# Attention and a two-layer MoE block on one core: another stored order for the same program

## The chip, the cores and the metric

The kernel runs on one core of one Trainium2 chip. The metric is the device time of one execution in microseconds; several executions are timed and their median is given. One further execution is recorded by the hardware profiler, and its page and trace are what this document reads.

## What is computed

Eight batches of eight heads attend over 576 tokens, each with a window of 128 keys back and a bias that grows with distance; the result of all heads, 4608 tokens of 512 values, goes through two matrices with `h * cos(h)` between them. The reference, cut:

```python
def _attn_ref(q, k, v):              # (8, 8, 576, 64)
    scores = scale * np.matmul(q, k.transpose(0, 1, 3, 2))
    bias = slopes[:, None, None] * (-np.abs(rel).astype(np.float32))[None, :, :]
    mask = (rel >= 0) & (rel < 128)
    scores = np.where(mask, scores + bias[None], -1000000000.0)
    ...
    return np.matmul(attn, v)
def _moe_ref(x, w_in, w_out):        # x (4608, 512), w_in (512, 2048), w_out (2048, 512)
    h = x @ w_in
    g = h * np.cos(h)
    return g @ w_out
```

## The kernel before

The program is a list of 2777 steps. A step is one or a few instructions of one engine; a step names what it reads and writes, and `Plan.op` (the planner's recording function) derives from that which earlier steps it must wait for. `Plan.emit` turns these into semaphore waits. What decides the order is `Plan.schedule`: it decodes a long text constant, `STARTS`, into one number for each step, sorts all steps by it, and so fixes the order of the instructions of each of the five queues (PE, ACT, DVE, POOL, SP). One bit of each number says which engine takes a step that may run on ACT or DVE. No time of the numbers is used on the chip: only their order.

```python
    def schedule(self):
        raw, n = zlib.decompress(base64.b85decode(STARTS)), len(self.all)
        ...
            o.start = code >> 1
            if len(o.eng) > 1:
                e = "dve" if code & 1 else "act"
                o.fn, o.eng = o.fn[e], (e,)
        self.order = sorted(self.all, key=lambda o: (o.start, o.seq))
```

The work itself has three interleaved parts.

*Attention*, unit by unit. A batch has nine units: four pairs of heads for each of two groups of 256 tokens, called G0 and G1, and a tail of 64 tokens. A unit's scores are matmuls (L497, tail L488) into PSUM banks 4 to 7; ACT takes the exponential (L529, tail L521); DVE multiplies by the mask (L553, tail L540); PE multiplies by v (L584 and L587, tail L571 and L573) into banks 2 and 3; DVE divides by the sum (L623 and L625, tail L610 and L613) into a ring of eight xnat buffers (two xtail buffers for tails). The result is transposed into xT, either on PE (L691, L653) with a copy by ACT or DVE (L700, L701), or by a DMA transpose on the SP queue (L714, tails L709).

The queries and keys of batches 0 and 1 are transposed on PE (L442, copies L459 and L460). Those of batches 2 to 7 are loaded by POOL into qnat and knat (L338) and then transposed by two DMA transposes each on the SP queue (L349 for the first 512 tokens, L352 for the rest) into qt and kt. Of all these there are two buffers, by even and odd batch, so the load for batch 3 onwards waits until the transpose before it has landed. v is loaded by POOL (L328).

*The first matrix (moe1)*: nine chunks of 512 tokens, numbered 0 to 8, each with 16 pieces of 128 outputs (L729; chunk 0 in halves, L753). A piece is four matmuls of 512 columns, a cosine on ACT (L735) and a product on DVE (L739) into gT. xT holds four batches' tokens and is used in a ring.

*The second matrix (moe2)*: chunk 0 plainly (L814, copies to the output buffers L820 or L822, stores L826). Chunks 1 to 8 use Strassen's seven products P1 to P7 of 16 matmuls each (L870) with sums of weights (L780) and of gT made by DVE, in banks 0 and 1. The partial results are read by ACT (L890) or DVE (L894) into four output buffers ob 0 to 3, in the order 0, 3, 2, 1, and each is stored by a DMA on the SP queue (L915). A buffer is written again only after its store has landed.

Three things set what waits for what around the change. Each engine takes its instructions strictly in the stored order. The SP queue carries three kinds of DMA in one order: transposes of q and k, transposes of xnat and xtail, and stores of outputs. POOL's queue carries all loads, in the order in which the program lists them, which the stored numbers do not move. At the start PE runs some matmuls on zeros (L415), ACT makes the masks (L422), and DVE sets constants with memsets (L393 to L398).

Of the kernel before, what the change touches and what calls it, by code (L numbers as in the profile page):

```python
# [14 lines left out]
B, H, S, D = 8, 8, 576, 64  # L15
# [12 lines left out]


STARTS = (  # L30
    "c-p;I4^&iD8lM5w+uPIjylD=XA&1L@)!DZ=!DE==&YKwm#u0JCBtYD7mURWuZ3#Cu{8JK=x<ux>u7#<cUH{g))KN}(j+SLb="
    "&I{6D{HsS&X)FPv&{tL&+K<+U>Fz>t8@09^WNP1-S7VSe&6r+-O*@$J(|9!uhpaVX*8odd>UV%3k|Km<KwSJ)7K1nq9P)@uL"
    "MRknm(tV{xt&zU!Oy8d|+1#zgn%PBkV-Mg-2{@hOqVA;CeSY+8we<r#3R^(-%g6-xty!7_)ESnr;5xs7Or&$3W9QI>M*DJUF"
    "6J?Sm~*or4UKn!!HWknQ_6^o4}c9byUh8SdLN7<OL>NWr!*1iFC%kGd8(ZkP5doDeea>(UOJzpw=KJ`p`5x`eMXx@|B(+Hg>"
    "MIBx#7HZ<FVvo@k7gc-hpx){V5txwxOldEkY-2NYa&WNtixxhZZTs7J@f1UwF&38sI{0VdE%~mMS!YrsG3`JiMzoAgP5nO#k"
    "(ait$1Pzf<SA%D03nsW1?$Mgip0=kmq8G6CfK}W5-O-5b8qp<8mzvR6ud{G}fL%kD8*O;u8Dj1a8r2R>m|j{!x_!Ovi0+V*&"
    "Y>977BX#g=eMJ{GP|$!7M@P+|A&x6#OE7I*4H8A^+h~P-P80FGJp^?BZAo<!)X@KY%c{PB0ECojryjShh5(Tgw7FN#)RD%H("
    "lu~dy##n&LM@X`3}PE9wr;17a{*fb#?b^xL<mmP=lcp+4eoO*gY~2dTzkd5mNR;Gab-g;M)_%fMG1!fd4?o@DR1yjuAr)OKQ"
    "}}A!={n-qTzi=HP*#`wo7+5H;7e0Jr(c!Y*ZB@Vvt--8V#3K5b`6yb=Dt3E^w_hOy;M@O?gkO4R>cPESlU=x$H{P;S@lYI2t"
    "Ddc^H^y4`h^$)7~kAHigf?{cxWO;@zz8OO%wzjivEwsiP_hugiz*6faRmFXwn{zy%nn*4_0(Fa%7I;FYtM|3y2H%&S#PM`j4"  # L40
    "aRgoZS2}mDLpqBy5?-Ek$o61k>B?DFv0b_)=_)O#IC|x$tCwtxzb_H#5fac^^-lu)ib7H?dr3eTA&i|Y7Ev=n0x=afA}=47^"
    "lZF<L~xaLES4aN&(*837-kTJ2zwM!FSLj`b1|5N1JbLdQ;!OKOh7tz(7&=E61EcwZYt!~>K=%}9)xXtv{2;3m6GoLGDScxO5"
    "{m1;v5NE7LLs~dvoWVp6`9(MC)=Q>hH)9FM484Ul{k#Z{2AY$*iB@tN9(XJ|`vn)_#>cI}L(NB_G5+tIYE?6gtF<%2=WyFG|"
    "1KbXVFqns9=Hc<G(d4d=YPHTK}o6TKU#OT^Wpl&%!u+eC~FmU>)+MWsZPptlQ)PWrIPDfZB<ISLld*p1I+B_^N6L@#0yJ4>*"
    "rrw58RxbvwZO6=FzB~n(1vALc-w7!}e*xq9o*5^3V<huX9sQ!W$87WIqJk-S2;bqEm>OEAUiRuE*4aZOB!<RiFiG;FKN)4W*"
    "9<8Eck~&_bGG&W5o8vua^$$&vGAAFD&3}>C&tIIK&Jt2qHE(a7V-+0<>ymTcYB-gK)r60vxALYyz%vCN<}%BcwSTvmkDRyYv"
    "mSGjN)M8G!V&-IE+-2Wi04obZ?ayAUKbogL=WjC?ybD1mwSx@ihYphmougoC8AYGm}tGghp1jaOOTw1>hf6XQvz~=EeZUJIL"
    "+2=F95tKJBURI0>j(zddHK-eNjrr-@J=(3457r!<*SH7~6^*zr$iVRUK5yDp2Dw#Yw7KMMM)TGrF*aO{bU`?rGdgFlCRI5F2"
    "Hyxev=e-SUj_kXd~Ict0cNXi}?e9-C7{=B5BA64FnSx{W)g8^>~n+(aVCwx*gNEqmMA+mlT>sU+9<a+)H&<4vHfRyN14*O?Q"
    "5UBzEo_8)TBx(}?-c^kb-i6y;6v-~qsX(yF3M+C!5jujwOArMRg7$wKOg@P~=&=X2bUICb;3*tDx=s*e+8~vk+V!3RVP?3P5"  # L50
    "?>GX2;wu)@9Y`LxLRhZdh>@9tE#;c{(o*WgL%0`3Y+$?LTd&T>`Bet>%VdgAI%ek=U^Dv|?D>v|M64+6BOtMveF_NO$^Hly%"
    "2Htko4Ot7ouux@P>?bngVazq26RBx<xiQ_+|x@_oGo|%o-F%7$w}M1J;U8@zhgzc**()#IWt9kx;_m{OV1fCH@7yJKjc;Coq"
    "5GZOIp)8vN{bU_nP+$3bc!=ZuLI@>K0SEWkW@LkW+z=&Hxy=poJ;W%!7pJ!#FS~1D+BuDd(F4=(;%3cr)g8?or^8?0g;=vNO"
    ";4nTb#lTHAoARJHQ$0wg6TfwcjXq`Eg0Dcbr83RE5glpv#o2u753V~d}{_3U+V$qG!}r|nPg-0YM96YxtA@&t<9l7YP@LX}f"
    "&pvSpz1{rD@WeWgMqfD@2>0U$yqdy&UAr8KWtnS4|B9~(^ku~zIU=KrPp>RNeVOT{?szP8h(#&jyvjWz0WN)iHwIkE2oE06e"
    "^DCOSpIG`!`hr+?q`{PP7x}0DJu8;1mnY)!cB3=(Wci*sQ$)S^aqFHl?h3c7c(*r;<GX+MIG3&3BNBlGP$c_Y=|U|D;w{E}C"
    "4{B`3%4gf>~CT?rGFNh_!5T%Rbr_1z&gPa9r+(*@=qW*Ij1#$3re-Zv9nA_vY|U6ym@lslhy_R4J4>=3QdzmslM#ZL(Mp!t+"
    "c<3J&wjnM9ez86lmtLE=a~8-$q_z*&0qf_8WdBvT2G7gx*%fS2*aW<s}i98`yh(&*@t%H|L6FDeG5Rb{b0BS2Z7RPH{lZ{dE"
    "7kN={7as>l>Nxl7eaR-0_TzxD<4_)KM=F}6}NTE_qOPCMiDbUd~4T1&1z-E{5i0W1WZfQL4yY=m<JqQcP!1E_GZAqjBN-IwG"
    "in;lpPWs;zA(U0@KOsWXM0xtm>$31*GjP<$r908WhTX4(WVi7RhLgc*W5`hXh+FC(5Q)W;XmeqAoyXx8Wrc&I+RxdKv)v1dW"  # L60
    "C69t|jV?fiDlS9gH*o#rs8cAlORSATft$M6WmBru$&^ZlsW*85z!`7a0KbJk!tb1!7n`>?zvMWRc%<y)DkW#l>DMxN=q`_R@"
    "5A>4iDqSc8x~boUD$W&{6!)m*~qib8LE3VP>^_d$VN>lW~#us+l!Jc6LR+^4v~>8A%r;j#UH&|Ksms7<U)3G&0cL>XuU#+M}"
    "{7%GQtm%qpf@73uG&)LY1(S;u5M;tuUR`&zPW)&6JhNn>>bDPudAE;Oh&;GR>awuXElCHLitvC#h>hSGALUD^aD1sT*4Wi8;"
    "&6HpB4;yq;y0EtCPLF~>y{Xf&m!N|6c=*X(yCF~z&-jMH*V+AYW)MC2BQQ=14Sq+CGWEU#TOKUeh`AvS&V^EH2l_$VzRHU%Q"
    "Xx|6bG<Pztoh#2?~x3U1@hssQlELKZ0er(z+e%4UIFI{+JthWhN){Bx~IG`jU+M0LXm9;CAmBYQxrqS|(MaSQ#MO!J0%-U+8"
    "RwyW+(YT|usm8$m0b4h)y_HG<EsMp9r}XeCdjTXelI+Jxj`0PrxD1ZM0_vepWVo=AX8*xM?FRL<w{}tW7SoR}QP3$4FqNOGC"
    "2uVz<P#T0&LVF`E0$?W-mMZ`1Q-|D6`ov0Z=@%b1A(-{faI-!W~6SGl2=h*wWoFigk3LdXlHzP{4p5jbL+V`k#Kav`w69h2G"
    "mEi$A6&-=+^ju$Nvukga^0"
)


# [988 lines left out]
```

The softmax here doesn't subtract the row's maximum and nothing guards it: scores larger than these inputs give would overflow.

## Time and profile before

| what | us |
|---|---|
| median of 6 runs (lowest to highest) | 305.74 (304.47 to 307.09) |
| the profiled execution, its own time | 306.38 |
| its span on the core | 304.7 |
| PE busy in the span, matmuls | 295.0 |
| DVE busy | 252.0 |
| ACT busy | 204.0 |
| POOL busy | 95.1 |

The span runs from the first to the last instruction that the profiler recorded; the 1.7 us between 304.7 and 306.38 lie around it. Times of single instructions below count from the start of the span. A group line of the profile gives the line of the kernel, engine, operation, tiles and shape, the count, the busy time, the mean of one in ns, and after the bar the idle time of the engine just before such an instruction with what ended it. A matmul's length in the profile holds its way through the pipeline, so back-to-back matmuls overlap in the list, and the distance of their starts is what a stream of them costs.

### The profile page before, as it was taken

The page shows a single profiled execution, that of the slowest core. Times are in us where ns is not written, and L with a number is a line of the kernel's source. Part 1 is how long each engine was busy: PE and PEld are TensorE (multiplying, and loading weights), DVE is VectorE, ACT ScalarE, POOL GpSimd, SP SyncE. Part 2 cuts the span into 40 slices and gives each one's busy share as a digit, 9 for nine tenths or more (in the row PEclk, how much of TensorE's full clock was granted, in tenths as well). Part 3 has the DMA queues.
Part 4 walks back from the last instruction along what each step waited for, and adds up shares of the span by engine and source line. Part 5 has one row for each costly group of instructions (what it writes and reads, how often), then busy time and mean ns, then how long its engine had stood idle before and what let it go on. Part 6 is the DMA issues. An engine that isn't in the chain of part 4 may idle for free.

```text
span 304.7 us, 7167 instructions
## 1 busy us (share of the span) xinstructions
PE 295.0 (97%) x2911; PEld 197.5 (65%) x2911; DVE 252.0 (83%) x542; ACT 204.0 (67%) x293; POOL 95.1 (31%) x122
## 2 busy tenths in 40 slices
PE   7699999998999999999999999999999999999996
PEld 3478745545874577537888886468645765555785
DVE  2788758789788998989988988999988976788963
ACT  6896877688555787787757776778667935556211
POOL 7998240052998801860178004000000000000000
PEclk9889999999999999999999999999999999999999
DMA  7999999999999999999899937960120314010044
GB/s 140 180 202 210 207 165 155 131 166 147 143 191 156 156 173 176 159 162 185 90 171 161 180 73 99 187 133 11 29 62 10 95 27 137 22 34 0 2 139 140
DMA packets 148353, 38.09 MB, mean 125 GB/s; under 512 B 133984, under 2 KB 147040, under 8 KB 148320
## 3 DMA queue, kind: packets, MB, share of 16 engines
q0 software_dynamic: 99344, 18.10, 76.1%
q1 hardware_dynamic: 48976, 19.54, 32.2%
q8 instruction: 23, 0.38, 0.6%
q14 instruction: 10, 0.08, 0.1%
HBM read 36.70 MB, written 9.44 MB: 151 GB/s over the span
## 4 chain that ended last, share of the span: by engine, by line
PE 87%; DMA 3%; ACT 3%; SPq 2%; DVE 2%; issue 1%; DVEq 0%
PE ps L870 32%; PE ps L729 32%; PE ps L497 5%; PE ps L753 5%; PE ps L814 5%; PE ps L584 3%; DMA kt<-knat 2%; PE ps L587 2%; ACT p L529 2%; SPq L349 2%; DMA ob<-in_q_dram 1%; PE ps L442 1%; PE ps L488 1%; PE ps L691 1%; PE ps L571 1%
## 5 line engine op out<-in xcount | busy, mean ns | idle before, releaser
L729 PE MATMUL ps<-xT,w_inb 128*128 128x512 bf16 (+1 forms) x576 | 129.7, 355 | 0.2
L735 ACT ACTIVATE cos<-ps,halfpi 128x512 f32<-128x512 f32 x128 | 83.0, 686 | 46.0 <-PE ps L729 32.9
L739 DVE TENSOR_TENSOR gT<-ps,cos 128x512 f16<-128x512 f32 x128 | 83.1, 686 | 15.2 <-ACT cos L735 14.4
L729 PEld LDWEIGHTS ps<-xT,w_inb 128*128 128x128 bf16 x576 | 54.5, 98 | 44.5 <-DVE gT L739 5.9
L529 ACT ACTIVATE p<-ps 128x768 bf16<-128x768 f32 (+1 forms) x64 | 56.3, 917 | 15.0 <-PE ps L497 12.8
L328 POOL DMA_DIRECT2D vp<-in_v_dram x40 | 34.0, 884 | 64.4 <-PE ps L587 53.4
L870 PE MATMUL ps<-wsum,gT 128*128 128x256 f16 x256 | 46.8, 273 | 0.0
L870 PE MATMUL ps<-wsum,gsum 128*128 128x256 f16 x256 | 46.1, 273 | 0.0
L553 DVE TENSOR_TENSOR p<-p,emask 128x512 bf16<-128x512 bf16 (+2 forms) x96 | 42.1, 459 | 4.0 <-ACT p L529 3.4
L870 PE MATMUL ps<-w_outb,gT 128*128 128x256 f16 x256 | 43.8, 273 | 0.0
L338 POOL DMA_DIRECT2D qnat<-in_q_dram x30 | 25.6, 900 | 18.9 <-DMA qt<-qnat 17.7
L870 PEld LDWEIGHTS ps<-w_outb,gT 128*128 128x128 f16 x256 | 24.9, 98 | 7.3 <-DVE ob L894 0.3
L338 POOL DMA_DIRECT2D knat<-in_k_dram x30 | 25.5, 913 | 9.5 <-DMA kt<-knat 8.1
L870 PEld LDWEIGHTS ps<-wsum,gT 128*128 128x128 f16 x256 | 23.7, 98 | 6.1 <-DVE krows L894 0.3
L870 PEld LDWEIGHTS ps<-wsum,gsum 128*128 128x128 f16 x256 | 23.4, 98 | 6.3 <-issue 0.8
L870 PE MATMUL ps<-w_outb,gsum 128*128 128x256 f16 x128 | 26.3, 273 | 0.0
L625 DVE TENSOR_TENSOR xnat<-ps,rec 128x256 bf16<-128x256 f32 x56 | 22.0, 419 | 0.5
L497 PE MATMUL ps<-qt,kt 64*128 64x128 bf16 (+1 forms) x320 | 19.2, 245 | 2.8 <-DMA kt<-knat 1.4
L584 PEld LDWEIGHTS ps<-vp,p 128*128 128x128 bf16 x256 | 16.1, 98 | 6.4 <-issue 3.7
L584 PE MATMUL ps<-vp,p 128*128 128x65 bf16 x256 | 18.5, 195 | 1.5 <-DVE p L553 1.3
L497 PEld LDWEIGHTS ps<-qt,kt 64*128 64x128 bf16 x320 | 11.3, 96 | 11.0 <-ACT p L529 3.0
L587 PE MATMUL ps<-vp,p 128*128 128x65 bf16 x192 | 17.3, 194 | 0.0
(78 smaller groups left out, 334.3 us busy)
## 6 DMA issues: line engine op xcount, KB each, us to landing
out_dram<-ob SPq DMA_DIRECT2D x32, 256.0 KB, 2.8
vp<-in_v_dram POOLq DMA_DIRECT2D x32, 128.0 KB, 7.5
qnat<-in_q_dram POOLq DMA_DIRECT2D x24, 128.0 KB, 8.9
knat<-in_k_dram POOLq DMA_DIRECT2D x24, 128.0 KB, 11.5
w_inb<-in_moe_w_in_dram POOLq DMA_DIRECT2D x4, 512.0 KB, 9.8
w_outb<-in_moe_w_out_dram POOLq DMA_DIRECT2D x4, 512.0 KB, 21.3
out_dram<-ob SPq DMA_DIRECT2D x8, 128.0 KB, 1.8
qrows<-in_q_dram POOLq DMA_DIRECT2D x1, 576.0 KB, 14.6
```

The lines of the kernel that those rows point to most:

```text
L328: op("pool", [lambda e, t=t, rows=rows: e.dma_start(vp[b % 2][0:rows, t, :, 0:64], v[b, :, 128 * t:128 * t + rows, :].rearrange("h p d -> ...
L338: fns.append(lambda e, t=t, rows=rows: e.dma_start(nat[which][b % 2][0:rows, t, :, :], src[b, :, 128 * t:128 * t + rows, :].rearrange("h p ...
L497: ins = e.matmul(ps[:, banks[x], c0:c1], keys_ap(b, x, pr, kc), query_ap(b, x, pr, qb, 128 * nb), start=True, stop=True)
L529: op("act", lambda e: e.activation(P[i][:, :, 0:hi], src_[:, :, 0:hi], ACTF.Exp, scale=0.125), w=held + [("P", i)], occ=920 if G else 691, ...
L553: op("dve", lambda e, p=p, m=m: e.tensor_tensor(p, p, m, ALU.mult), r=[("P", i), ("EM", h0), ("EM", h1)], w=[("P", i)] if n != 1 else [("P ...
L584: ins = e.matmul(o, P[i][:, x, d0:d0 + 128], V[:, kc, h, 0:65], start=True, stop=not two)
L587: ins = e.matmul(o, P[i][:, x, p0:p0 + 128], V[:, kc - 1, h, 0:65], start=False, stop=True)
L625: op("dve", lambda e: e.tensor_tensor(o, U[:, :, :, 0:64], rv[:, :, :, None].broadcast_to([128, 2, 2, 64]), ALU.mult), r=[("rec", n % 2)], ...
L729: op("pe", lambda e, kc=kc, c0=c0: e.matmul(ps[:, bank, c0:c0 + n], w_in[:, kc, 128 * fc:128 * fc + 128], xT[:, kc, (r0 + c0) % XR:(r0 + c ...
L735: op("act", lambda e: e.activation(cosb[ci][:, :], ps[:, bank, :], ACTF.Sin, bias=halfpi[:, 0:1]), r=["halfpi"], w=[("B", bank), ("cos", c ...
L739: op("dve", lambda e: e.tensor_tensor(gT[gi][:, fc, :], ps[:, bank, :], cosb[ci][:, :], ALU.mult), r=[("cos", ci)], w=[("B", bank), ("g", ...
L870: op("pe", lambda e, t=t, fc=fc, bk=bk: e.matmul(ps[:, bk, 256 * t:256 * t + 256], lhs(fc, t), rhs(fc), start=first and fc == 0 and (last ...
```

## The change

Only the constant `STARTS` is replaced. All 2777 steps, their instructions, buffers, sizes and dependencies are the same. The search that made the new numbers charged half a semaphore latency more for each hand-over from one engine to another.

```diff
 STARTS = (
-    "c-p;I4^&iD8lM5w+uPIjylD=XA&1L@)!DZ=!DE==&YKwm#u0JCBtYD7mURWuZ3#Cu{8JK=x<ux>u7#<cUH{g))KN}(j+SLb="
...
+    "c-oy-3s_Xg72dm`j<=1uPHbI<4X(rG;d&tiuW;e+0}$4Q$cmca79+0sB1kI5JQN5~LmtJgQQQ&}Ok!SIE76d&B$|FUNo{<@R"
...
```

The text of the constant says nothing to a reader; what it decodes to does. Fifteen evacuations that may run on either engine go from ACT to DVE, eight go from DVE to ACT. The order of POOL is the same. PE, ACT, DVE and SP have other orders nearly everywhere, though the coarse sequence of stages is kept. The two stretches of the SP queue of which the prediction speaks, in short names (T2q is the transpose of batch 2's queries, XDt1 the tail of batch 1, XD60a the xnat transpose of batch 6, head pair 0, group G0, and b for G1; ST0.4 the store of buffer 0 of chunk 4; 2p1 the store of chunk 0's tile 1):

```
before: XDt0 T2q XDt1 2p1 2p0 2p3 T2k 2p2 T3q ST3.1 ST0.1 T3k T4q ST1.1 T4k
after:  XDt0 2p1 2p0 T2q T2k 2p2 XDt1 2p3 T3q T3k ST0.1 T4q ST3.1 T4k

before: ST3.3 XD52a ST0.4 XDt4 XD42b XD50a XD51a XD43b ST2.3 XD50b XD53b T7k ST2.4 ST1.4 XD52b XD51b T7q ST3.4
after:  XD43b XD52a ST3.3 ST3.4 XD52b XD60a ST1.3 T7k XD51b ST2.4 T7q XD61a XD53b XD50b ST0.4 ST1.4
```

At the start, the steps of DVE and ACT up to the copies of the first keys (L460, L459):

```
DVE before: memset L412, L393, cast L320, memsets L395 L394 L398 L393, qt, memsets L396 L398 L394, kt
DVE after:  memset L412, L393, cast L320, memsets L395 L398 L394, qt, kt
ACT before: 3 masks, copy L321, 3 masks, qt, mask, kt, mask
ACT after:  3 masks, copy L321, 5 masks, qt, kt
```

The memsets that are no longer there stand later on DVE. On DVE, after, the sum of chunk 4 for buffer 3 (L894) stands after the norm of batch 6's first unit. In moe1 and moe2 the matmuls of neighbouring pieces and products are mixed in other proportions, and the scores, PV products and transposes of single units stand up to about 3 us of PE work earlier or later.

More of the change, by code (lines that the diff above doesn't have):

```diff
@@ L30 @@
 STARTS = (
-    "c-p;I4^&iD8lM5w+uPIjylD=XA&1L@)!DZ=!DE==&YKwm#u0JCBtYD7mURWuZ3#Cu{8JK=x<ux>u7#<cUH{g))KN}(j+SLb="
[L32 to L65, printed above, removed]
@@ L66 @@
-    "RwyW+(YT|usm8$m0b4h)y_HG<EsMp9r}XeCdjTXelI+Jxj`0PrxD1ZM0_vepWVo=AX8*xM?FRL<w{}tW7SoR}QP3$4FqNOGC"
-    "2uVz<P#T0&LVF`E0$?W-mMZ`1Q-|D6`ov0Z=@%b1A(-{faI-!W~6SGl2=h*wWoFigk3LdXlHzP{4p5jbL+V`k#Kav`w69h2G"
-    "mEi$A6&-=+^ju$Nvukga^0"
+    "c-oy-3s_Xg72dm`j<=1uPHbI<4X(rG;d&tiuW;e+0}$4Q$cmca79+0sB1kI5JQN5~LmtJgQQQ&}Ok!SIE76d&B$|FUNo{<@R"
+    "%*?wCfa<7wkBz!Muh;o+jE!K?y`W%eBaKUIdkT5{`t>8t75z!RbT0Ac^I#nVXt(n-M%i=UX|C|Q$elj?faK-b(s6Is&};K<M"
+    "pjKu(~p-&!K<ZJ20Z`!@x=^ReS#wx8LO8Q;uW{HR>ML?|S!e4@BYZV#4~}2BHq^LwHPZ%-(=C!>;(&9nGlKjMC}~W4z2IRd8"
@@ new lines @@
+    "{uMk;DmN3bcpTNS*ahZ$JS?KkT0;~lp41cB4n^aQlMjF;(c1qB@5*>l`(rX4O_v39GNz;k<p1Mv(B)-$3@c-J6HFhESNkJk?"
+    "lWgQ0EjIRzplV=FaP++N4-T+4UC4%oWh#^5a)OS#5k7*Csxl`TK0u+52$&Ad9K@bJw9?B*7E*Pe3&>G%BD0+KQRE0#*?YH?*"
+    "xP}bJ2aKm5q42JL^nEv}?)Fc>fS%gjr2yttdzcQ0!J}fl?vX+rj0Q6@?M8JD;%YDvnK9Qw?CHKv`BDu#S9P5$4?j9!8SU=uZ"
+    "!=-v4><bbbo(J3##|Yt=$Yqx6{A4UbTL1ekf>v1LVB)48$+fwqZ*Qsp5ZM_NZsovWN%sr5;9C-AJeT&_Vnfm6F^Tz{+J&5`@"
+    "uXMtZjo_*lWRQimnVn=TM2ugiO<+EJG$P(}#@8U);j_kKgIz3ZwcFxj4FWL>{QSM`q9H%fkv#&vW3r!M+zXz=sL>1h@m3#6Y"
@@ new lines @@
+    "}^XXI-hWC$C1&UGb7dx(GnRGJA4V)(Y(FCF@7ui6`8XHWm5<msi2XOMz=LfpQG>GqGM_jH~RScI|_O!R&=k@D16E~dxE>NHX"
+    "5XT^&b#m?IDgR8C946F6p=H%8A`}xgZI=a3sV%jzK%ngShJ9H)^Bg2pmmE8*EglDJos3o7|M7?aEoMSl7<xV*|=WhKf%O(1@"
+    "c6ufzhFfCWh>E_sSlE-6DxSjT%$G9Prfm5uzw4z;?!QaFA|iRU=<O>rHfHhBQVnZD;wHUj;km>rf>?y=<d+e_*ot^f&SwNsE"
+    "D=<Zwh@C3Q$ZvD5An#(vB*CEVTviZBCYWTjwKvoiALVd2_i-=lC|I{uG>&p#9B1+VQ|v098NU;1QGZm@cXj?_QHjP$e+WWti"
+    "Ax1t;)n4Hi#@rls~4}23Dkz*YE$!pG?fc-0w=4w>3LzUDB$eD(%xNHNU58X-Cvjy)^NiM$_LGaEG|X<oK-#HLaiD_h1fxip!"
@@ new lines @@
+    "t;J~7#!fBnm4srVWnLDZ338+MWWRLsZKD<Hb}lnVDbl-B$$N47cAacKhw@re{~#&8UsWiH2qfm;VLiWsNkMVav&7A=(y0plX"
+    "f6&>2-N&d*f3ED~u{weS9n3k^|Ux&e8UN3T(rp*?p<dpAa4`Q9X+j8pQ^Ye0?MQwGnw_<A7$%|mCMENilv!6FVih&XGuc*jT"
+    "dF&dI@WvJ@K>GsVL*<8g0~U<Cc#hX)-r*{VsrrDVPQ&JevwA6R%@@MrTkwq7?X|6Oi4#+?IlAe^&ECqZY23`{6a0MgUFrn7H"
+    "QQ<}u^#N+<e1)2`NldaDQO9cDs~}(DEF<Puer!3qsHEjQbm4`{CZGnDoyakD3Q%ZS|9+6Bko2pNsve-Vkt(khKMCj@YRAdl~"
+    "~Rci#kqREeFR8jI2aiC&OlqsU{re=*%|(+W6bfnk=~9{GfQ8hUc%=t7*aPXKB&)jNF?5(4slN=6F#jKMr@0m7hr|A8%d;H$g"
@@ new lines @@
+    "KW#Ui~&J}rt^cgI~K<!EM1p-8E53)};hb59<r*6t+>65!Tj$T#s(%a3i<9<xl7C2i?z#2&Y*wzZ`>+RUHAIof|s-IbgdUBAf"
+    "3kSI^&v&oJzq>AJKNiO6~(uA$k+ioV@UZb+s;_kV#tc}(+(l*D+%SYO_Ntegn90(E8=-3Q_!z{pq3`jEZ^3A>xto$$qyC!*b"
+    "zzoF3tYA4`3)`XohDDKStqRUy;~q=IoFt-AuU#pJE)Q$qN*J2(%j$b)VTc}RhM~S6yqxBl9KNq!{tr$Px63bNi6$yv#UjU>s"
+    "}(95&tfdXaR4E`dACAuc_QXY^>T|IFw0qy?E;!j#oWO}^AkKrV&(bUq)2U4&OGU@JEzUu-I<)%()OGDtPZ;Dtp+jg#*fI=82"
+    "r#1sW@f5S}#38j#+*?9RM{8g?cI1@d0U?&UNrz@y9S^*V0+r93ML3rQ-B>>3s(Q(t%8n9#k~Pc_h{K;N!z1?c)G+v_f)iH;W"
@@ new lines @@
+    "+Q5Gv66_=n;iV)ax(2bW+Z<RNyFcS4Uh&PdKfCZ~mccu@*CYO`6CWz#2G=B{zgyMLXs2PhAfx5Dn=46T*ESqMAj+e$#i3aYj"
+    "X#v96E<gy)z6oV5%s7g#a`7}`u&@-399FEl)n=r0GrAl_jfOrA_A?uq!43(qnjE5=WVVkx}V>ORN1mWuBKZ?Xel+i_>SxP}w"
+    "L0K2Bf=dMx>^A3_yeaoAG|%0c@nGW_F)uQE?MnWDe%~txfuPi`b<g1Wb3n;|exjFN6UvGnN&tkXIvmJaWnEspt3lm(Qc4P+^"
+    "GPWHJOH5v^3+h^>tP?l5tn*9Jw67lhAoCKK}pa}_t_#ogjztyd?pr^);yV3<MS@3>#PI|VyA0b+IEwLRFHbYl7E{h`v-RN>H"
+    "~NKC|CqhRI3TwvYfel$YTvVjcMGA!Yui;9^W%dZg(UrPXJY@8)wPJdB#scW2roz!-W6E3{Zy3v#S+($V?c=0kU%}kk<<qa~4"
@@ new lines @@
+    "cz=0BD4GZMdS8f4;4q$9Dm^=ey_`KjWM79EOBvA$4K*Ak8QG^Y~7`kIm>Q#U!uu3G@0vA6$SFU_}}EPGGM;IYC2$+h9<lH;V"
+    "&;Alk-($6z;F@;5C1mQlMrd${xA!Z5HYR>P47Y<E8$fTHn50THopdJ&p5pzJzBosLY_tBOhg9$%Uu;+$XVKr?!NFuIbE&3ge"
+    "390o&iEp1T1tUQO>*aky8Qv_f<Q!iX8)piMfX7{srYYv9;kBXiGMoZ0$qEjHFYR^km&`f%U0h)N6jtEP`?AXv{6ukYrEwA#1"
+    ";A<C=5rP24s%PnmfBb`FE^<=_0DGLj-?#`06CgFAur}c`i^m5OT|eMaLEvnQujRp$WTRaKYMQd%wMMfm#D^AkSdUNfh9I2O~"
+    "|CJz2n(@#@=#bdgSdB^?DYO3W4y=Kn@!LIkWP}=0Z+ndQlJz0w%ZZZ{|7Cx#V%dvP0N1Q6M1l>n%jMQ+^*yg`#}FsS)2UZ*="
@@ L69 @@
+    "_>GVcL{v-Jx(g4df;<Q69g*^@6(Y3EXTl#|;~yl);BEDiFFRY1Kt|A6IVn-XmH3M#*wezN&M`hgFgLw2}Zmb4;#8D4HmlHe("
+    "~P>7nPpdT!WctF4w10p5^i%iP>k_li%B1;Kt5NvQX92o=NrI6p+Su8P_D%gm$^N6z4W@Gg=AR6#@W=h(57WF6^=E0QWh)Aoj"
+    "xX3f|{xVwVG+#>QIjL#M8vZRhJI*Fj*0_puET>1;iiFn4sn<BIPWDn)6_ppdOa>}f+k|c^=TMuVliS<)3OalLQ`<Rep1c=3&"
+    "Sbt^hzn!QXWrRi3zr<OZw-njVl2Q9)!~${lRgnpiXFt|K#4#cqQIXveMkgBad0#e-!puS3bf6~VuZg@o^lYN_X;j>Wh^ZrWs"
+    "L%<I}iWh-dk}Y`gck^z_XpKkMekY^tosW5ng%BUV)@l$TBwi+vxuTNm3!G"
 )
```

## Prediction, made before the changed kernel was run

> **What bounds the kernel now.** I read the page's busy shares and costliest groups first, then the chain that ended last, then the waits of TensorE and of the DMA queue SP around the one place where the chain leaves TensorE. From the page, the busy shares and two groups (busy us, mean ns of one, idle before):
>
> ```profile
> PE 295.0 (97%) x2911; PEld 197.5 (65%) x2911; DVE 252.0 (83%) x542; ACT 204.0 (67%) x293; POOL 95.1 (31%) x122
> ...
> L729 PE MATMUL ps<-xT,w_inb 128*128 128x512 bf16 (+1 forms) x576 | 129.7, 355 | 0.2
> L870 PE MATMUL ps<-wsum,gT 128*128 128x256 f16 x256 | 46.8, 273 | 0.0
> ```
>
> 97% says nothing about what is left: the mean of 355 ns holds each matmul's pipelined end. What matters is the distance from start to start, which the chain shows (start us, us, what):
>
> ```profile
> 59.29 0.70 DVE gT L739
> 59.99 1.22 SPq L709
> 61.21 0.04 issue
> 61.25 0.58 SPq L826
> ...
> 62.84 4.80 SPq L349
> 67.64 0.04 issue
> 67.68 6.56 DMA kt<-knat
> 74.24 0.05 issue
> 74.29 0.50 PE ps L497 x8
> ```
>
> Near its end the whole-span chain has 155 matmuls of L870 in 17.08 us, 110 ns each, and at 191.33 fifty of L729 in 10.79 us, 216 ns each. I listed every start-to-start distance on TensorE and took off what the same pair of steps takes where nothing waits (the lower fifth of its kind). Left over after 20 us are only 4.5 us: 1.5 us in one piece at 74.29 and 3.0 us in many pieces, the largest 0.3. From 10 to 20 us 3.0 us are lost in the start-up. So TensorE in program order sets the time, and an order can win a few us at most. The piece at 74.29 on TensorE, and the SP queue that made it:
>
> ```profile
> 72.57 0.27 PE L870 MATMUL ps<-wsum,gsum 128*128 128x256 f16 x1
> 74.29 0.50 PE L497 MATMUL ps<-qt,kt 64*128 64x256 bf16 x8 [1.45 <-DMA kt<-knat]
> ```
>
> ```profile
> 48.91 5.09 SPq L349 DMA_TRANSPOSE qt<-qnat  x1
> 54.04 1.25 SPq L352 DMA_TRANSPOSE qt<-qnat  x1
> 59.23 1.98 SPq L709 DMA_TRANSPOSE xT<-xtail  x1
> 61.25 1.55 SPq L826 DMA_DIRECT2D out_dram<-ob  x3
> 62.84 4.80 SPq L349 DMA_TRANSPOSE kt<-knat  x1
> 67.68 1.34 SPq L352 DMA_TRANSPOSE kt<-knat  x1
> ```
>
> SP stood from 55.29 to 59.23 on the tail transpose of batch 1 (L709). The chain puts DVE's gT ahead of it, but L709 began at 59.23, 0.03 us after DVE's last tail product (L613) ended at 59.20: that was its releaser. The keys of batch 2 had landed at 52.91 but were behind it, with three stores. They came transposed at 74.24, 1.5 us too late.
>
> [...]
>
> **The change part by part.** Instructions and buffers stay. The order shows new places on PE, ACT, DVE and SP; POOL's is the same. 23 evacuations change engine, 15 to DVE and 8 to ACT (ACT 277 to 270 steps, DVE 542 to 549).
>
> *Batch 2's transposes, SP.* After: tail of batch 0, the stores of plain tiles 1 and 0, queries, keys, and only then store 2, batch 1's tail, store 3. The two stores need copies that ended at 44.39 and 46.38; one position later in the new ACT order is some 46.5, and two issues at 0.5 end before 48.9, when the queries land. Queries 48.9 to 55.3 as now, keys 55.3 to 61.5, landing 5.2 to 6.5 later: 67 to 68. TensorE asks at 72.8. Gain 1.5. Bounds: 0 (if something else is late there) to 1.6; I take 1.5. What is late next are the PSUM banks of those scores: by the durations of the cos and gT rows they are free 0.2 us before PE asks. The moved tail is wanted at 89.8, store 2's buffer at 92: covered.
>
> *What follows on POOL and SP.* The key load of batch 3 waits for that landing (74.53 now), so it and the loads behind it come up to 7 us sooner. Batch 4's key transposes now land at 119.14 for scores at 120.42; the new order asks about 1.2 us of TensorE work sooner. With earlier loads they land near 110. Bounds 0 to 2.4 us lost (if loads stay late); I take 0.
>
> *Other moves on SP.* In chunk 3 the transpose of batch 4's first unit (issued at 137.19 now) stands behind one whose data exist at about 146: it lands at 150 to 154 and moe1 asks at 153.4. Bounds 0 to 1; 0, as landings there took 1.5 us after issue (148.47 to 151.32). The last eight stores keep their order, so the 3.1 us from the last matmul's start (301.58) to the end of the span stay.
>
> *Start-up.* Three memsets (0.5 us, rows at 7.34 to 7.90) leave the place ahead of DVE's key copy, but ACT does five masks (0.34 each) ahead of its own instead of three. Key copies end near 8.25 instead of 8.61. Later the piece of keys that lands at 10.57 bounds both orders, so of 0.4 I take 0.3; bounds 0 to 0.8. Above 1.2 us there is nothing: the second w_in piece landed at 19.88 for use at 21.12. Moving the memset of the second v buffer to about 18.7 delays POOL's load issue by 1.2 us; those loads land 24 us after issue, so the backlog hides it.
>
> *Tighter or looser hand-overs.* For each PE step that needs a DVE or ACT result I counted the PE work (30 ns a PV matmul, 110 and 216 as above) between the last matmul that feeds the result and the step, less the durations of the chain's rows and 45 ns a hand-over. Between start-up and the last chunk 82 of them have under 0.2 us left in the old order and 45 in the new; 16 are short by 1.4 us in sum, after the change 3 by 0.3. I take the difference, 1.1 us, out of the 3.0 measured; bounds 0 to 2.5. In the last chunk both orders are about equally short and little was measured: 0. Table switches stay 15. DVE's seven extra copies at 0.3 to 0.7 us are under 3 us in 305, beside PE.
>
> *A new tight place, SP in chunk 5.* The store of output buffer 0 of chunk 4 was issued at 176.98. It now stands behind batch 7's transposes and six xnat transposes, and chunk 5's first output (ACT L890, 207.6 now) writes that buffer. SP first waits for the store of buffer 3, whose sum DVE now does after the norms of batch 6's first unit. That unit's PV (188.89 now) is 2.4 us of PE work earlier, and 2.9 by the gains: 183.6, plus 2 for masks, norm and sum queued on DVE: 185.7. Then store 0.5, two transposes 2.6, store 0.5, keys 5.1 (as at 187.51 to 192.60), transpose 1.3, store 0.5, queries 3.4 (as at 197.17 to 200.57), three transposes 3.9, store 0.5: issued by 204.0, landed 1.9 later, 205.9. ACT wants it at 207.6 less 2.9: 204.7, and PE has 0.2 of cover before the product that needs the bank. Loads are done sooner in the new order, so the keys may take 3.4 too: 1 us late to 0.7 early. I take 0.4 lost; bounds 0 to 7.
>
> Sum: 1.5 + 0.3 + 1.1 - 0.4 = 2.5 us. The profiled execution took 306.38 with a span of 304.7; the span becomes 302.2. The median of six was 305.74, so 303.2.
>
> **The rivals.**
> - *More:* PE's small gaps fall by twice as much and the new place costs nothing: 1.5 + 0.5 + 2.2 = 4.2, 301.5. For it: half the tight places are gone. Against: many gaps are short and DVE at 83% queues.
> - *Eaten:* transposed keys come early, but the SP queue gives most of it back in chunk 5 or at batch 4 (2 us), 305.2. It includes that the order does little where PE is already fed, which speaks for it: only 3.0 us were there to win.
> - *Slower:* the store of buffer 0 behind batch 7's transposes. If these take what batches 3 and 4 took (7.9 and 6.6 us) instead of 5.1 and 3.4, it lands 6 us later: ACT stands at L890, the exponentials behind it and PE's next product with it, 7 us lost against 2.9 won, 309.8. It decides from 3.1 us of lateness. For it: the issue is 27 us later than now, with no room. Against: those slow ones ran beside loads; by 190 the last loads are in.
>
> **How the numbers follow.** Forecast (302.2 to 304.2) 0.45; more 0.15; eaten 0.25; slower 0.15. A measurement of this kernel can tell about 0.5%, 1.5 us, from no change, so faster is below 304.2: 0.60; same 0.25; slower 0.15. The range from 301.3 takes in the larger gain, and reaches to 306.8 into the slow case; 0.04 below and 0.15 above are left out.
>
> **What would show it.** Right: no idle time of PE before the batch 2 scores near 72, keys of batch 2 issued near 55.3; fewer small gaps; ACT's L890 in chunk 5 waiting under 1 us. Wrong: a DMA of out_dram ending a wait of ACT near 205; a wait of DVE or PE for xnat transposes; batch 4's scores waiting for kt near 117; a start-up no shorter.

## The result, and the profile after

| | before | after |
|---|---|---|
| median (lowest to highest), us | 305.20 (303.92 to 307.09), 66 runs | 304.58 (303.79 to 306.88), 29 runs |
| ratio of after to before, 95% interval | | 0.9984 (0.9972 to 0.9996) |
| the profiled execution, its own time | 306.38 | 304.31 |
| its span | 304.7 | 302.6 |

The new order wins 0.5 us by the ratio (0.6 between the medians), where 2.5 were forecast. The two profiled executions are 2.1 us apart, close to the forecast; the medians are not. The profile shown of before was 1.2 us slower than the median of its kernel, the one of after 0.3 us faster than its own. So part of what I read in that one profile was not typical of the kernel, and the first thing to find out was which part.

From the page of after, the busy shares, the matmul group shown before, and the weight loads of the same line with what ended their waits:

```profile
PE 292.8 (97%) x2911; PEld 199.6 (66%) x2911; DVE 254.9 (84%) x549; ACT 200.8 (66%) x286; POOL 95.1 (31%) x122
...
L729 PE MATMUL ps<-xT,w_inb 128*128 128x512 bf16 (+1 forms) x576 | 130.8, 355 | 0.0
...
L729 PEld LDWEIGHTS ps<-xT,w_inb 128*128 128x128 bf16 x576 | 55.5, 98 | 39.3 <-DVE gT L739 1.1
```

The last line in before, from the same list:

```profile
L729 PEld LDWEIGHTS ps<-xT,w_inb 128*128 128x128 bf16 x576 | 54.5, 98 | 44.5 <-DVE gT L739 5.9
```

The waits at moe1's weight loads that a product of DVE (gT) ended have fallen from 5.9 to 1.1 us. The place of the old stall, first the SP queue and then TensorE (start us, us, engine, line, operation):

```profile
51.26 5.35 SPq L349 DMA_TRANSPOSE qt<-qnat  x1
56.65 1.25 SPq L352 DMA_TRANSPOSE qt<-qnat  x1
57.95 6.43 SPq L349 DMA_TRANSPOSE kt<-knat  x1
64.42 1.25 SPq L352 DMA_TRANSPOSE kt<-knat  x1
```

```profile
72.88 0.38 PE L870 MATMUL ps<-wsum,gsum 128*128 128x256 f16 x2
73.19 0.50 PE L497 MATMUL ps<-qt,kt 64*128 64x256 bf16 x8
```

The keys of batch 2 follow the queries at once and land at 66.92, and the scores at 73.19 wait for nothing: the mechanism is as forecast. Chunk 5 is not. The chain that ended last now runs through SP there (start us, us, what):

```profile
195.76 2.42 SPq L349
198.18 0.04 issue
198.22 1.35 SPq L352
199.57 0.04 issue
199.61 1.25 SPq L714
200.86 0.04 issue
200.90 1.25 SPq L714
202.15 0.04 issue
202.19 1.25 SPq L714
203.43 0.46 issue
203.89 2.50 DMA out_dram<-ob
206.39 0.02 issue
206.41 0.61 ACT ob L890
207.01 0.05 issue
207.06 0.61 PE ps L870 x4
```

Queries of batch 7, three xnat transposes, then the store of buffer 0, which lands at 206.39 and lets ACT's L890 begin. In the timelines of ACT and of TensorE the waits stand in brackets:

```profile
206.41 0.60 ACT L890 ACTIVATE ob<-ps 128x512 f32<-128x512 f32 x1 [1.47 <-DMA out_dram<-ob]
```

```profile
207.06 0.61 PE L870 MATMUL ps<-wsum,gsum 128*128 128x256 f16 x4 [1.15 <-ACT ob L890]
```

ACT stands 1.47 us and TensorE 1.15, where the forecast took 0.4 lost. At the start TensorE waits twice for pieces of w_in, which it did not in before:

```profile
20.45 1.49 PE L753 MATMUL ps<-xT,w_inb 128*128 128x256 bf16 x12 [0.45 <-DMA w_inb<-in_moe_w_in_dram]
```

```profile
26.42 2.36 PE L753 MATMUL ps<-xT,w_inb 128*128 128x256 bf16 x20 [0.39 <-DMA w_inb<-in_moe_w_in_dram]
```

Distances from start to start on TensorE, less those of the same pair of steps where nothing waits, sum up after 20 us to 4.55 us in before and to 3.18 in after; such a sum is called the gaps below. Of the 3.18, 1.22 are at 207 and 1.17 at the two pieces of w_in.

### The profile page after: what moved, and what is told of

Same layout as the page of the kernel before. It is cut to its first block, busy times and chain, and to the rows that moved or that the text cites. A ratio compares the mean times of both kernels' runs of the same rounds, so it can differ in the third digit from the quotient of the medians.

```text
span 302.6 us, 7152 instructions
## 1 busy us (share of the span) xinstructions
PE 292.8 (97%) x2911; PEld 199.6 (66%) x2911; DVE 254.9 (84%) x549; ACT 200.8 (66%) x286; POOL 95.1 (31%) x122
## 4 chain that ended last, share of the span: by engine, by line
PE 81%; DMA 7%; SPq 6%; DVE 2%; ACT 2%; issue 1%; POOL 0%
PE ps L729 32%; PE ps L870 30%; PE ps L814 5%; DMA w_inb<-in_moe_w_in_dram 5%; PE ps L497 4%; PE ps L753 3%; SPq L714 2%; PE ps L584 2%; SPq L349 2%; PE ps L587 2%; DMA ob<-in_q_dram 1%; SPq L352 1%; DMA out_dram<-ob 1%; PE ps L442 1%; PE ps L488 1%
## 5 line engine op out<-in xcount | busy, mean ns | idle before, releaser
L729 PE MATMUL ps<-xT,w_inb 128*128 128x512 bf16 (+1 forms) x576 | 130.8, 355 | 0.0
L729 PEld LDWEIGHTS ps<-xT,w_inb 128*128 128x128 bf16 x576 | 55.5, 98 | 39.3 <-DVE gT L739 1.1
L870 PE MATMUL ps<-wsum,gT 128*128 128x256 f16 x256 | 48.3, 273 | 0.0
L870 PE MATMUL ps<-w_outb,gT 128*128 128x256 f16 x256 | 42.0, 273 | 0.0
L870 PE MATMUL ps<-w_outb,gsum 128*128 128x256 f16 x128 | 27.3, 273 | 0.0
L753 PE MATMUL ps<-xT,w_inb 128*128 128x256 bf16 x128 | 16.1, 273 | 1.7 <-DMA w_inb<-in_moe_w_in_dram 0.8
```

The lines of the kernel that those rows point to most:

```text
L729: op("pe", lambda e, kc=kc, c0=c0: e.matmul(ps[:, bank, c0:c0 + n], w_in[:, kc, 128 * fc:128 * fc + 128], xT[:, kc, (r0 + c0) % XR:(r0 + c ...
L753: op("pe", lambda e, i=i, fc=fc, kc=kc: e.matmul(ps[:, bank, 256 * i:256 * i + 256], w_in[:, kc, 128 * fc:128 * fc + 128], xT[:, kc, r0:r0 ...
L870: op("pe", lambda e, t=t, fc=fc, bk=bk: e.matmul(ps[:, bk, 256 * t:256 * t + 256], lhs(fc, t), rhs(fc), start=first and fc == 0 and (last ...
```

## The experiments

The first four kernels ask which of these pieces are in typical executions. All but the hybrids below leave the stored numbers as they are and move single steps in the sorted list:

```diff
-        self.order = sorted(self.all, key=lambda o: (o.start, o.seq))
+        self.order = sorted(self.all, key=lambda o: (o.start, o.seq)); [(self.order.remove(self.all[s]), self.order.insert(self.order.index(self.all[t]) + d, self.all[s])) for s, t, d in (...)]
```

A triple (s, t, 0) puts step s ahead of step t, (s, t, 1) behind it. Every run of the kernel before that was made beside an experiment is in the "before" of that ratio; its medians were 304.79 to 304.96.

**Both kernels once more (b_same, a_same), no edit.**

> The kernel before, unchanged, once more: a second profile of it, and what the comparison gives for equal kernels. Theory A (the profile shown of before is typical of it): TensorE again waits about 1.5 us for the transposed keys of batch 2 near 74 us, and the span is near 304. Theory B (the stall of 1.5 us comes only in the slower executions, and the one profiled at 306.38 was one of them): here the wait before these scores is under 0.7 us or absent and the span is nearer 303. Both: ratio 1.000 within 0.002.

> The changed kernel, unchanged, once more. If what its profile shows is typical, TensorE again waits some 1.0 us in two pieces for the pieces of w_in at 20 to 27 us and 1.2 us for output buffer 0 at 207, and the keys of batch 2 are in time; ratio to before 0.998 as measured. If the lost gain is spread otherwise, one of these waits is absent or differs by over 0.5 us.

Measured: b_same 304.70, ratio 0.9996 (0.9979 to 1.0013); a_same 304.15, ratio 0.9985 (0.9966 to 1.0004). In the second profile of before (its own time 304.59, span 302.9) the stall isn't there. The transposes of the keys, and TensorE at the scores:

```profile
61.85 3.58 SPq L349 DMA_TRANSPOSE kt<-knat  x1
65.47 1.40 SPq L352 DMA_TRANSPOSE kt<-knat  x1
```

```profile
72.32 0.27 PE L870 MATMUL ps<-wsum,gsum 128*128 128x256 f16 x1
72.58 0.51 PE L497 MATMUL ps<-qt,kt 64*128 64x256 bf16 x8
```

The SP order is the same, the keys are issued a microsecond sooner, the first transpose holds SP 3.58 us instead of 4.80, and they land at 72.01 instead of 74.24: 0.6 us ahead of TensorE. From there on the two profiles of before run in parallel to the end, 1.8 us apart, with spans of 302.9 and 304.7. Theory B holds. In the second profile of after the wait for buffer 0 is there again (TensorE 1.21 us); its two waits for w_in after 20 us are not, but there is one of 0.86 us at 15.95 and one for a piece of v:

```profile
18.83 0.21 PE L584 MATMUL ps<-vp,p 128*128 128x65 bf16 x1 [1.27 <-DMA vp<-in_v_dram]
```

So the wait for buffer 0 belongs to the order, and the start-up differs from execution to execution.

**Keys first, in the kernel before (b_keys): (399, 391, 0).**

> The kernel before with one step moved: the key transposes of batch 2 stand ahead of the tail transpose of batch 1 on the SP queue, instead of behind it and three stores. Nothing else is moved. Theory A (the stall at 74 us is in every execution of before): 1.5 us less, ratio 0.995, about 303.7. Theory B (only in the slower executions): under 0.5 us less, ratio 0.998 to 1.000. If the gain is given back by the tail transpose coming later: slower, 1.000 or more.

Measured: 304.70, ratio 0.9995 (0.9975 to 1.0015). The keys land at 62.85, ten microseconds before they are wanted, and the median doesn't move by anything that can be told. That is theory B; theory A's 0.995 is outside the interval. The text before the run named a third way, that the gain is given back by the tail transpose, which now comes later. It isn't: compared at equal amounts of TensorE work, this profile is never more than 0.15 us from the second profile of before, from 10 us of work to the end.

**Two more profiles of before (b_look1, b_look2), no edit.**

> The kernel before, one more look. The wait for the keys of batch 2 was 1.5 us in the profile shown, 0 in the second, 0.6 in the third with this order up to there. Theory B (it varies with the time that the key transposes take, 6.2 against 5.0 us, and with their landing): a value from 0 to 1.5, with the landing time of the keys less 72.7 us as its size, and the span 302.9 plus that wait within 0.4.

> The kernel before, a further look, for the same count: theory B expects a wait between 0 and 1.5 us equal to the landing time of the keys less 72.7 us, and a span of 302.9 plus the wait within 0.4.

Measured: spans of 303.8 and 303.0. In the first the keys were issued at 61.90 and 66.59 and TensorE waited:

```profile
73.49 0.50 PE L497 MATMUL ps<-qt,kt 64*128 64x256 bf16 x8 [0.79 <-DMA kt<-knat]
```

In the second TensorE did not wait: the scores began at 72.66, when the keys had just landed. The waits of the four profiles of before are 1.45, 0, 0.79 and 0 us, their spans 304.7, 302.9, 303.8 and 303.0: the span is 302.9 plus the wait, to 0.4 us. The keys arrive within a microsecond or so of the moment at which they are needed, on either side of it.

**The store of buffer 0 moved ahead (a_store), in the changed kernel: (1684, 1719, 0).**

> The changed kernel with one step moved: the store of buffer 0 of chunk 4 stands ahead of the store of buffer 3 of the same chunk, so that batch 7's transposes and six xnat transposes no longer stand before it. If the wait of 1.2 us at 207 us is in typical executions: 1.2 us less than the changed kernel, about 303.4, ratio to before 0.994. If in typical executions the store just lands in time, or something else is late there at once: 0 to 0.3 us less, ratio 0.997 to 0.998.

Measured: 303.05 in 7 runs, ratio 0.9932 (0.9908 to 0.9956). That is 1.1 us less than the changed kernel beside it (304.15), and 1.5 less than in the first comparison (304.58). Its profile has no wait of ACT for a store; the output at the same place:

```profile
204.13 0.60 ACT L890 ACTIVATE ob<-ps 128x512 f32<-128x512 f32 x1
```

```profile
204.95 0.61 PE L870 MATMUL ps<-wsum,gsum 128*128 128x256 f16 x4
```

One step of 2777 in another place on SP's queue is worth more than all that the change wins, and with it the changed order is 1.9 us faster than before. After 20 us its profile has 0.96 us of such gaps in all, against 3.00 in the profile of before in which the keys were in time: 2.0 us, which I put down to the hand-overs. Along TensorE's stream, that is at equal amounts of TensorE work done, the profile of a_store moves from 0.1 us ahead of that profile at 22 us of work to 2.4 ahead at the end: 2.3. Whether the order alone does this, or also the 23 evacuations that changed engine, no run separates.

**The fifth piece of v behind w_in (a_v04: (35, 60, 1)), and both moves (a_both: (1684, 1719, 0), (35, 60, 1)).** POOL issues its loads in the list's order, so the last piece of v of batch 0 goes behind the last three pieces of w_in, ahead of which it stood.

> The changed kernel with one load moved: on POOL the fifth piece of v of batch 0 is loaded behind the last piece of w_in, instead of ahead of the second. Theory C (what the changed kernel loses in the start-up are its waits for w_in, 1.0 us at 20 to 27 us): each piece of w_in is asked for 0.5 us sooner, 0.5 to 1.0 us less than the changed kernel, ratio to before 0.995 to 0.997. Theory D (the start-up differs from execution to execution by what the loads deliver, whichever is first): no difference, 0.998. If that piece of v is late instead: 0.999 or more.

> The changed kernel with two steps moved: the store of buffer 0 of chunk 4 ahead of that of buffer 3, and the fifth piece of v behind w_in. Theory C: the two gains add up, 0.5 to 1.0 us less than with the store alone (303.05): 302.0 to 302.6, ratio 0.990 to 0.992. Theory D: as with the store alone, 0.993.

Measured: a_v04 303.48, ratio 0.9960 (0.9941 to 0.9978); a_both 302.79, ratio 0.9914 (0.9891 to 0.9938). Alone it reads 0.7 to 1.1 us better than the changed kernel (304.15, 304.58), on top of the store 0.26 better; both intervals overlap with those of the kernels without the move. Both ratios are in the ranges of theory C; theory D's 0.998 lies just outside the interval of a_v04, its 0.993 inside that of a_both. Yet the profile of a_both still has a gap of 0.96 us for w_in, at 26.32. So these two lean to theory C and don't settle it. The profile of a_v04 has a wait that none of after had, for the transposed keys of batch 4:

```profile
118.80 0.41 PE L488 MATMUL ps<-qt,kt 64*128 64x64 bf16 x16 [1.39 <-DMA kt<-knat]
```

There they land at 118.76; in the profile of after they landed at 117.59 and were in time.

**Hybrids: the order of one kernel up to a step, then that of the other.** Each step is taken with the engine that its own order gives it; the numbers are stored anew.

```diff
-order = after
+order = before[:211] + [o for o in after if o not in before[:211]]   # a_start
+order = a_start, with (1684, 1719, 0)                                # h_start
+order = before[:766] + [o for o in after if o not in before[:766]], with (1684, 1719, 0)   # h_late
+order = after[:766] + [o for o in before if o not in after[:766]]    # h_early
```

The start-up of before, without and with the store moved:

> The changed kernel with the start-up of before (its first 211 steps, up to 24 us of PE time), nothing else: the late store of buffer 0 stays. If the new start-up loses about 0.5 us in the median, as the profiles say (0.9, 1.9, 0 against 0 to 0.25 with the old one): 303.9, ratio to before 0.996. If the start-up costs nothing in the median: as the changed kernel, 304.4, 0.998. If it is a gain, as forecast: 304.7, 0.999 or more.

> The order of before up to 24 us of PE time (its first 211 steps), then the order of the changed kernel, with the store of buffer 0 of chunk 4 moved ahead. It tells what the new start-up is worth. Theory C (the new start-up loses 0.5 to 1.5 us on average, the rest of the new order without the late store wins 2.3): 302.5 or less, ratio 0.990 to 0.992. If the new start-up costs nothing on average: as the changed kernel with that store moved, 0.993. If it is a gain as forecast (0.3): 0.994.

Measured: a_start 304.31, ratio 0.9981 (0.9963 to 0.9999), the same as the changed kernel; h_start 302.63, ratio 0.9917 (0.9897 to 0.9937), the same within the intervals as a_store. So the new start-up shows neither the gain of 0.3 nor a loss that these runs could tell, though profiles of it reached 22 us of work 0 to 1.9 us later than that of before. a_start also has the wait for buffer 0, h_start doesn't, and they are 1.7 us apart. The line of a_start:

```profile
206.97 0.61 PE L870 MATMUL ps<-wsum,gsum 128*128 128x256 f16 x4 [1.48 <-ACT ob L890]
```

The last two thirds and the first third of the change:

> The order of before up to 93 us (its first 766 steps, start-up and batch 2 with them), then the order of the changed kernel, with the store of buffer 0 of chunk 4 moved ahead. It tells what the hand-overs after 93 us are worth by themselves. By the PE stream of the profiles, 1.5 us between 100 and 150 us and 0.7 after 195 us: 302.8, ratio 0.993. If they were worth the 1.1 us of the forecast, in all of the program: 304.0 or more, ratio 0.9965.

> The first 766 steps of the changed kernel's order (start-up, batch 2's transposes, to 93 us), then the order of before. What the first third of the change is worth. By the forecast: 1.5 for the keys and 0.3 for the start-up, with 0.2 of hand-overs: 2.0 us less, ratio 0.9935. By the sum of parts as measured since (start-up 0.5 lost, keys 0.4 won in the median, hand-overs 0.3 won): 0.2 us less, ratio 0.998 to 1.001.

Measured: h_late 303.57, ratio 0.9954 (0.9937 to 0.9970); h_early 304.42, ratio 0.9987 (0.9970 to 1.0003). The first third, with the early keys and the new start-up, wins nothing that can be told: the forecast's 2.0 us (0.9935) are outside the interval. h_late lies between its two expectations. Its profile suggests why; at 304.23 this execution was 0.7 us slower than the median, so what it shows need not be typical. Two waits for keys, of batch 2 as in before and of batch 4,

```profile
73.11 0.50 PE L497 MATMUL ps<-qt,kt 64*128 64x256 bf16 x8 [0.55 <-DMA kt<-knat]
```

```profile
118.61 0.41 PE L488 MATMUL ps<-qt,kt 64*128 64x64 bf16 x16 [0.75 <-DMA kt<-knat]
```

take back 1.3 us; without the one at batch 4, the hand-overs after 93 us are worth some 1.7 along the stream.

**Aiming at the best order (best_start, best_v04).** SP stands idle for 7.4 us ahead of the query transposes of batch 4 (88.54 to 95.98 us in the first profile of after), and one store whose data are ready stands behind them. Both kernels move it ahead, (736, 638, 0), beside what h_start and a_both have.

> As the kernel with the start-up of before, the rest of the new order and the store of buffer 0 of chunk 4 ahead (302.63), and with the store of buffer 3 of chunk 1 ahead of the query transposes of batch 4, where SP stood idle. The key transposes of batch 4 are then issued 0.6 us sooner. If in some executions these keys still come late (1.45 us in the profile of the kernel with v moved, 0 in five others): 0.1 to 0.4 us less in the median, 302.2 to 302.5, ratio 0.991. If not: 302.6 as before.

> The changed kernel with three steps moved: both stores as in the run beside it, and the fifth piece of v behind w_in, with the new start-up. 302.3 to 302.8, ratio 0.991. If the batch 4 keys were late in typical executions, 0.4 us less than with two steps moved (302.79); otherwise the same.

Measured: best_start 303.14, ratio 0.9945 (0.9925 to 0.9965); best_v04 302.72, ratio 0.9929 (0.9905 to 0.9953). No gain over h_start and a_both; best_start's 0.991 lies outside its interval. The five orders with the store of buffer 0 moved and the rest of the new order from 24 us on lie between 302.63 and 303.14 with intervals that overlap: all beat both kernels, 0.55 to 0.86% below before, and which is best can't be said. The plainest is a_store.

## Why the prediction was wrong, point by point

*What bounds the kernel.* Right: TensorE in program order sets the time (busy for 295.0 and 292.8 us of spans of 304.7 and 302.6, with gaps after 20 us of 4.55 and 3.18), and only a few microseconds are to be won.

*Batch 2's transposes, 1.5 us.* The mechanism is right and was seen; the size failed. "Gain 1.5. Bounds: 0 ... to 1.6; I take 1.5" took the wait of one profiled execution for the wait of the kernel. That execution was slower than the median because of this wait: over four profiles it is 1.45, 0, 0.79, 0, and curing it alone moved the median by 0.25%, 0.8 us, at most by its interval (b_keys). I wrote that the profiled 306.38 stood beside a median of 305.74 and subtracted all the same the whole stall from the median. The difference was the warning: a gain that is read in a profile which is slower than the median has to be checked against that surplus.

*Store of buffer 0, 0.4 lost.* The place, the path and the order of the queue were right, and so was the walk: it had the store issued by 204.0 (203.89 measured), landed at 205.9 (206.39: the landing took 2.5 us, not 1.9) and ACT asking at 204.7 (204.94). By my own numbers that was 1.0 us late for TensorE after 0.2 of cover. I then let the keys be fast enough to be 0.7 early, and took 0.4. Batch 7's transposes held SP 4.0 us for the keys and 3.8 for the queries, faster and slower than I had it, and the sum came out at the walk's value. The runs put it at 1.1 to 1.7 us (a_store against the changed kernel, h_start against a_start), and TensorE stood 0.9 to 1.5 us for it in each of the four profiles that have the new order there and the store where that order puts it.

*Hand-overs, 1.1 gained.* The direction is right, the size too small: 2.0 by the gaps and 2.3 along the stream (a_store). The model's 45 ns a hand-over was of the measured size (in the chain above 20 ns from the landing to ACT and 50 from ACT to TensorE), but its shortfalls (1.4 us before, 0.3 after) explained only about half of the 3.0 us that were measured, and I took their difference as it stood. The share that it removed, 1.1 of 1.4, applied to the measured 3.0 would have given 2.4. This gain is the steady one: the waits of L729's weight loads for gT are 5.9 us in three profiles of before (the first, b_same, b_look1) and 1.1 in five of the whole new order (the first, a_same, a_store, a_both, best_v04).

*Start-up, 0.3 gained.* The mechanism was seen, the gain was not. The first scores begin at 8.14 and 8.20 us in the two profiles of after, against 8.51 to 8.75 in the four of before, but this lead is gone by 22 us of work, after waits for loads. The first profile of after is 0.9 us later there than the second of before, the second one 1.9 later, that of a_store 0; the runs with the start-ups exchanged show no difference (304.31 against 304.15 and 304.58). What differs from execution to execution is which load comes late, w_in or v, and when, if at all, the granted clock falls to 0.50 for 3.4 us (last section). Whether the new start-up costs or gains something on average stays open: each of these ratios is known to 0.2%, some 0.5 us, either way. Moving one load did not settle it.

*Batch 4's keys, 0.* "With earlier loads they land near 110" is wrong: they landed at 117.59, 1.5 us sooner than in before, because batch 4's query transposes waited for their load until 95.98 and the keys stood behind them and a store. They are now as close to their moment as batch 2's were: in time in most profiles, 1.39 us late in that of a_v04 and 0.75 in h_late.

*The sum.* The forecast was 1.5 + 0.3 + 1.1 - 0.4 = 2.5. What the runs show is 0 to 0.8 for the first term, nothing that can be told for the second, 2.0 to 2.3 for the third and 1.1 to 1.7 lost for the last. So the steps that failed are the first term and the last: together they were put at 1.1 us won, where the runs show 0.3 to 1.7 us lost. That the third was too small hid part of this. These terms add up to between 0.3 and 2.0 us won; 0.5 was measured (0.1 to 0.9 by the interval), near the lower end. With the store moved they add up to between 2.0 and 3.1, and 1.9 was measured. Of my rivals "eaten" came closest, for the first of its two reasons: SP's queue gives the gain back in chunk 5, and in some executions at batch 4. That its 0.5 us won (305.2 from 305.74) is the measured value is in part luck, since it counts the keys at 1.5 and the hand-overs at 1.1. Its second reason, that order does little where TensorE is fed, is refuted by a_store. Three of the four signs of being wrong that the prediction named came: a store ended a wait of ACT near 205 (206.41), batch 4's scores waited for kt (in a_v04 and h_late), and the start-up was no shorter.

## What to carry to other kernels

A wait for a DMA in one profile is a sample (here 1.45, 0, 0.79 and 0 us in four profiles of one kernel): look at the same place in several executions before its whole length goes into a sum, above all when the profiled execution is slower than the median. A wait between engines that comes from the order alone can be counted once where it repeats: here those for gT were 5.9 us in three profiles of before. And where a walk along a queue gives a value, take it; the kinder case belongs in the range (here 1.0 us late by the walk, 0.4 taken, 1.1 to 1.7 measured).

## What the runs showed of the hardware that was not expected

In the first profiles of before and of after TensorE's matmuls on zeros (L415, 512 columns) start 427 ns apart from 1.66 to 4.65 us, twice the 216 of later ones. The view gives a clock of 1.00 there, but the clock records of the two begin only at 6.53 and 6.72 us. After that the granted clock falls to 0.50 for one stretch of 3.4 us in twelve of the sixteen profiles, and not in the others. Its place moves. The stretches of the first profile of before (from and to in us, length, then busy time with instructions of PE, PEld, DVE, ACT and POOL, granted clock, DMA share, GB/s), and then those of the second profile of after:

```profile
10.00:12.00 2.00, 1.36 (x28) 0.81 (x28) 1.97 (x5) 2.00 (x4) 2.00 (x4) 1.00 2.04 173
12.00:14.00 2.00, 1.03 (x18) 0.72 (x18) 1.97 (x8) 1.45 (x3) 2.00 (x4) 0.84 1.31 200
14.00:16.00 2.00, 1.97 (x29) 1.42 (x27) 1.66 (x8) 1.46 (x2) 2.00 (x3) 0.50 2.36 158
16.00:18.00 2.00, 1.64 (x30) 1.15 (x29) 2.00 (x6) 2.00 (x5) 2.00 (x4) 0.81 1.30 208
```

```profile
18.00:20.00 2.00, 1.17 (x18) 1.14 (x19) 0.10 (x1) 0.98 (x2) 0.03 (x1) 0.70 1.27 205
20.00:22.00 2.00, 2.00 (x13) 1.47 (x12) 1.78 (x6) 0.35 (x1) 1.17 (x2) 0.50 1.24 206
22.00:24.00 2.00, 2.00 (x31) 1.81 (x30) 1.17 (x4) 1.99 (x3) 2.00 (x3) 0.95 1.24 211
```

In the latter the matmuls of 256 columns are 213 ns apart instead of 109 between 20 and 22 us, and the stretch comes with the end of the wait for v quoted above: these, with the wait for w_in at 15.95, are how its start-up came to be 1.9 us late. The profile of after shown first has no such stretch. Such a stretch halves the clock over about a hundredth of the span (3.4 of some 303 us), so a run's mean clock tells of it, 0.994 (or 0.993) against 1.000 (or 0.999). Among the 106 runs of before beside the experiments 34 had 1.000, with a median of 304.15, and 69 had 0.994, with 304.99. The new order had 1.000 in 20 of 44, with 304.14, and 0.994 in 20, with 304.70; the few others of both had 0.988 or 0.989. Some of the spread of the medians goes with this. At equal clock the two kernels are 0 and 0.3 us apart, so some of the 0.5 us between them goes with it too; whether the new order meets the stretch less often, or did so here by chance, is not shown. What calls it up is not settled: in most profiles with such a stretch a wait of TensorE of 1.1 to 1.6 us stands ahead of it, but the four without one also waited 1.1 to 1.2 us at 12 us and kept the full clock. Why waits of equal length go with a stretch in one profile and not in another is not shown. The stretches are equally long: the clock record of the first profile of before has 3.413 us, from 13.35 to 16.77, after 6.827 us at 1.00, and the views of the other eleven come to 3.4 us each.

The same DMA transpose of 512 tokens, at the same place of the same queue, held SP for 3.58 to 4.82 us in four executions of one kernel, and the second transpose landed 5.8 to 6.8 us after its issue began. In the profile of after, where the last loads had landed by 187.06, those of batch 7 held SP 2.69 and 2.42 us.
